# A chunk's results as running totals: 38 additions for 34, six PSUM copies for eight

## The chip, the cores and the metric

The kernel runs on one core of a Trainium2 chip. The metric is the device time of one execution in microseconds. The kernel before takes 1823.01 us, the median of three runs (1822.85 to 1823.12). Five engines of the core work side by side: TensorE (PE) multiplies matrices, VectorE (DVE) and ScalarE (ACT) work element by element and can read PSUM, GpSimd (POOL) works element by element in SBUF, and SyncE (SP) issues the DMAs.

## The reference, cut to what matters

```python
X = np.fft.fft(x, axis=1)          # x: 8 x 3008 x 256, float32
X = np.fft.fft(X, axis=2)
x = X.real.astype(np.float32).reshape(24064, 256)
h = x @ w_in                       # 256 -> 2048
g = np.maximum(0.01 * h, h)
return (g @ w_out).astype(np.float32)   # 2048 -> 256
```

## The kernel before, in words

The transform along the sequence is written with cosine and sine tables and folded by its symmetries. Each of the 8 batches gives two units, one with the odd and one with the even frequencies. The transform along the 256 features is folded into `w_in` (tensor `wf`). A unit is cut into two chunks of 188 or 189 pairs of columns; the first unit has one chunk of 125 pairs and is preceded by some plain pieces. So there are 31 chunks.

**Up.** A chunk takes 16 up steps, one for each block of 128 of the 2048 hidden features (`Chunk.up`, L1111). In a step TensorE makes a cosine product and a sine product (L1114) into the PSUM banks `cos_ps` and `sin_ps`, of which there are two each. ScalarE copies the cosine product (L1120) and writes the next start value into the bank (L1109). VectorE makes the sum and the difference of the two (L1127, two operations a step), which are the hidden values of both columns of a pair, and ScalarE applies the leaky ReLU (L1386).

**Down.** The product with `w_out` is not made block by block. Sums of hidden values (`SUMS`, L1144, on GpSimd or VectorE) are multiplied by sums of weights (`wt`, made once), as in fast matrix multiplication. A chunk has 26 products of four matmuls each (`PRODUCTS`, L1165); they accumulate to 24 values, numbered 0 to 23. Value a lies in half a % 2 of a PSUM bank, and a chunk fills 12 banks in order, in a ring of three (`sum_psa`, `sum_psb`, `sum_psc`). The products of a chunk run among the up steps of the next one.

**Results.** Eight results of 128 x 188 are signed sums of the 24 values. The table `COMBINED` lists additions `(x, y, sign)`. Entry i makes value 24 + i from two earlier ones; `RESULTS` names the eight that are stored. Values in `COPIED` are first copied from PSUM to SBUF by ScalarE (`combine`, L1181). All others are read by VectorE straight out of PSUM until their last use, and only then the bank is free. Every addition runs on VectorE (`make`, L1210) and writes to one of 24 slots of `part`. It has either two SBUF operands or one in PSUM.

**The order of the work.** It is fixed when the program is built. `rest` (L1298) sorts events by due time: up steps, sums and products. At each event `some` (L1331) hands out VectorE time from a budget in microseconds, first to the additions that are ready (`make_some`, L1223), and then to the folds of the next units' input and transform, which stand in one queue (`folds`, `Later.emit`, L983). The folds' operations have the lines L958, L960 and L978. An addition costs n / 960 + 0.07 of the budget. If products need a bank that still holds unread values, `leave` (L1194) emits the missing additions at once. A chunk's transform must be complete before its unit's first up step: `mixc` and `mixs` are the moving operands of L1114.

An addition from SBUF alone is also noted in `gate`. GpSimd's next sum is made to wait for the latest one noted (`wait_for_gate`, L1009).

The last chunk has its own tables, since none follows it.

Of the kernel before, what the change touches and what calls it, by code (L numbers as in the profile page):

```python
# [80 lines left out]
    (24, 7, 16), (25, 6, 17), (8, 39, 18), (13, 40, 19), (2, 8, 20), (1, 41, 21), (12, 42, 22), (5, 43, 23),  # L81
]
COMBINED = [
    (0, 12, -1), (20, 22, -1), (1, 10, 1), (6, 9, 1), (14, 19, -1), (11, 26, -1), (15, 27, 1), (3, 7, 1), (18, 24, 1),
    (12, 29, 1), (8, 31, 1), (25, 32, 1), (28, 34, 1), (2, 7, 1), (36, 20, 1), (38, 21, 1), (6, 4, -1), (40, 33, -1),
    (30, 3, -1), (42, 17, -1), (43, 25, -1), (13, 33, -1), (45, 36, -1), (14, 23, 1), (47, 35, 1), (1, 5, 1), (49, 37, 1),
    (50, 27, 1), (37, 30, 1), (52, 35, -1), (26, 0, -1), (54, 13, 1), (55, 16, -1), (56, 28, -1),
]
RESULTS = [39, 41, 44, 46, 48, 51, 53, 57]
COPIED = [0, 1, 2, 3, 4, 6, 14, 20]  # L90

LAST_COMBINED = [
    (0, 12, -1), (1, 10, 1), (6, 9, 1), (14, 19, -1), (11, 25, -1), (15, 26, 1), (3, 7, 1), (18, 24, 1), (12, 28, 1),
# [2 lines left out]
    (50, 27, -1), (14, 31, 1), (47, 31, -1), (41, 20, -1), (52, 20, 1), (53, 20, -1), (55, 22, -1), (54, 22, 1), (56, 22, 1),  # L96
    (57, 23, 1),
]
LAST_RESULTS = [37, 39, 58, 43, 60, 46, 59, 51]
NA = 24  # L100

# [193 lines left out]
def tile_fnet_leaky_relu(  # L295
# [792 lines left out]
    class Chunk:  # L1088
# [3 lines left out]
        def __init__(self, t):  # L1092
# [3 lines left out]
            self.last = t == len(chunk) - 1  # L1096
            self.combined, self.results = (LAST_COMBINED, LAST_RESULTS) if self.last else (COMBINED, RESULTS)
            self.sum_left = [0] * (NA + len(self.combined))
# [75 lines left out]
        def combine(self, bank):  # L1174

            n, here = self.n, [a for a in range(NA) if self.place(a)[0] == bank]
            for a in here:
                self.ready.add(a)
                if a in COPIED and not (self.last and a == 20):
                    self.copy[a] = part_of.take()  # L1180
                    nc.scalar.copy(part_of[self.copy[a]][:, 0:n], self.in_bank(a))  # L1181
                else:
                    self.held.add(a)
            for i, (x, y, _) in enumerate(self.combined):
                v = NA + i
                if v not in self.ready and x in self.ready and y in self.ready:
                    self.ready.add(v)
                    self.open.append(v)
# [446 lines left out]
```

## Time and profile before

| what | value |
|---|---|
| median of three runs | 1823.01 us |
| the profiled execution | 1822.73 us |
| its span, first to last instruction | 1820.9 us |
| TensorE busy | 1814.2 us |
| VectorE busy | 1550.7 us |
| ScalarE busy | 1124.1 us |
| GpSimd busy | 1081.9 us |
| additions, L1210 | 1057 on VectorE |
| copies, L1181 | 247 on ScalarE |

In the views of the profile, a row of a group gives line, engine, operation, what is written and read, shapes and count, then busy time, mean duration in ns, and the engine's idle time just before. A row of the timeline begins with start and duration in us, and ends with the count of merged instructions and, in brackets, an idle time and what ended it. In the waits, the numbers are the total in us, how often, and the longest. Each float32 matmul shows as two rows, since it is made in two passes, so 4712 matmuls give 9424 rows.

### The profile page before, as it was taken

To read this page: it belongs to the slowest core of one execution; us is meant where nothing else is said; L and a number is where in the kernel's file an instruction comes from. 1 tells how busy PE (TensorE), PEld (TensorE's weight loads), DVE (VectorE), ACT (ScalarE), POOL (GpSimd) and SP (SyncE) were. 2 spreads that over 40 slices of the span, in tenths; PEclk is the share of its full clock that TensorE was granted. 3 is DMA by queue.
4 is the path that set the end of the run, shared out by engine and by line. 5 is a ranking of instruction groups with operands and counts; after the bars stand their busy time and mean duration, and the time that the engine had idled before them with its cause. 6 is when DMAs were issued, how large, how long until landed. Compare 5 with 4: busy or idle time off the path is not lost.

```text
span 1820.9 us, 27090 instructions
## 1 busy us (share of the span) xinstructions
PE 1814.2 (100%) x9424; PEld 1543.4 (85%) x9424; DVE 1550.7 (85%) x3223; ACT 1124.1 (62%) x2297; POOL 1081.9 (59%) x587
## 2 busy tenths in 40 slices
PE   9999999999999999999999999999999999999999
PEld 7888888888888888888888888888888888888888
DVE  8979998897888978899787988879888798887678
ACT  4558666675666756566565666657666576565551
POOL 0246666565666665666665666656666666666660
PEclk9999999999999999999999999999999999999999
DMA  6312121202012011121101112010121110010000
GB/s 237 119 48 90 30 69 34 73 14 72 30 28 73 20 66 31 29 70 35 58 25 31 68 35 73 18 68 24 33 72 35 52 30 28 25 35 13 10 18 31
DMA packets 65897, 88.61 MB, mean 49 GB/s; under 512 B 10064, under 2 KB 53456, under 8 KB 65760
## 3 DMA queue, kind: packets, MB, share of 16 engines
q1 hardware_dynamic: 65616, 86.88, 14.5%
q8 instruction: 74, 1.21, 0.3%
q14 instruction: 63, 0.52, 0.1%
q10 hardware_dynamic: 144, 0.00, 0.0%
HBM read 62.12 MB, written 24.72 MB: 48 GB/s over the span
## 4 chain that ended last, share of the span: by engine, by line
PE 96%; DVE 2%; issue 0%; POOL 0%; DMA 0%; ACT 0%; DVEq 0%; POOLq 0%
PE sum_psc L1165 21%; PE sum_psa L1165 17%; PE sum_psb L1165 17%; PE cos_psa L1114 9%; PE sin_psa L1114 9%; PE sin_psb L1114 8%; PE cos_psb L1114 8%; PE dft_ps L713 3%; PE sum_psa L939 1%; PE sum_psb L939 1%; PE dft_ps L939 1%; PE sum_psc L939 1%; DVE block L1144 1%; PE sin_psb L901 0%; PE cos_psb L901 0%
## 5 line engine op out<-in xcount | busy, mean ns | idle before, releaser
L1144 POOL TENSOR_TENSOR block<-block 128x752 f32<-128x752 f32 (+2 forms) x540 | 1045.8, 1949 | 608.5 <-DVE xt L960 175.6
L1386 ACT ACTIVATE block<-block 128x376 f32<-128x376 f32 (+5 forms) x718 | 426.5, 623 | 3.9 <-DVE block L1127 3.2
L1144 DVE TENSOR_TENSOR block<-block 128x752 f32<-128x752 f32 (+2 forms) x328 | 417.4, 1276 | 0.2
L1127 DVE TENSOR_TENSOR block<-cos,sin_psa 128x376 f32<-128x376 f32 (+2 forms) x510 | 250.5, 531 | 141.6 <-PE sin_psa L1114 136.6
L1165 PEld LDWEIGHTS sum_psc<-block,wt 128*128 128x128 f32 x1736 | 289.3, 189 | 45.8 <-issue 0.5
L1165 PE MATMUL sum_psc<-block,wt 128*128 128x188 f32 (+2 forms) x1736 | 327.3, 321 | 0.4 <-DVE part L1210 0.4
L1127 DVE TENSOR_TENSOR block<-cos,sin_psb 128x376 f32<-128x376 f32 (+2 forms) x482 | 239.9, 538 | 101.1 <-PE sin_psb L1114 99.8
L1165 PE MATMUL sum_psa<-block,wt 128*128 128x188 f32 (+2 forms) x1736 | 312.1, 321 | 0.0
L1165 PEld LDWEIGHTS sum_psa<-block,wt 128*128 128x128 f32 x1736 | 283.4, 189 | 22.8
L1120 ACT COPY cos<-cos_psa 128x376 f32<-128x376 f32 (+2 forms) x255 | 119.0, 467 | 250.0 <-PE cos_psa L1114 247.2
L1120 ACT COPY cos<-cos_psb 128x376 f32<-128x376 f32 (+2 forms) x241 | 113.6, 471 | 210.8 <-PE cos_psb L1114 210.7
L1114 PE MATMUL cos_psa<-mixc,wf 128*128 128x376 f32 (+2 forms) x510 | 199.8, 473 | 0.5 <-ACT cos_psa L1109 0.5
L1114 PE MATMUL sin_psa<-mixs,wf 128*128 128x376 f32 (+2 forms) x510 | 199.7, 473 | 0.0
L1114 PE MATMUL sin_psb<-mixs,wf 128*128 128x376 f32 (+2 forms) x482 | 191.5, 479 | 0.0
L1114 PE MATMUL cos_psb<-mixc,wf 128*128 128x376 f32 (+2 forms) x482 | 191.4, 478 | 0.0
L1210 DVE TENSOR_TENSOR part<-part 128x188 f32<-128x188 f32 (+2 forms) x462 | 187.5, 442 | 1.8
L1165 PE MATMUL sum_psb<-block,wo 128*128 128x188 f32 (+2 forms) x992 | 188.0, 321 | 0.0
L1165 PEld LDWEIGHTS sum_psb<-block,wo 128*128 128x128 f32 x992 | 165.2, 189 | 22.8
L1165 PEld LDWEIGHTS sum_psb<-block,wt 128*128 128x128 f32 x992 | 163.5, 189 | 22.8
L1165 PE MATMUL sum_psb<-block,wt 128*128 128x188 f32 (+2 forms) x992 | 176.9, 321 | 0.0
L1109 ACT ACTIVATE cos_psa<-nb,wn 128x376 f32<-128x376 f32 (+2 forms) x255 | 146.0, 572 | 8.2
L1114 PEld LDWEIGHTS sin_psa<-mixs,wf 128*128 128x128 f32 x510 | 96.5, 189 | 61.8 <-DVE block L1127 0.4
(213 smaller groups left out, 1953.6 us busy)
## 6 DMA issues: line engine op xcount, KB each, us to landing
xt<-in_x_dram SPq DMA_DIRECT2D x28, 1024.0 KB, 5.3
out_dram<-part SPq DMA_DIRECT2D x176, 94.0 KB, 1.7
out_dram<-part SPq DMA_DIRECT2D x64, 94.5 KB, 1.7
tabe<-in_seq_tab_dram SPq DMA_DIRECT2D x29, 190.0 KB, 2.6
nb<-nyq_dram SPq DMA_DIRECT2D x23, 188.0 KB, 3.8
block<-in_w_in_dram SPq DMA_DIRECT2D x8, 512.0 KB, 5.4
block<-in_w_out_dram SPq DMA_DIRECT2D x8, 512.0 KB, 4.6
xt<-in_first_x_dram SPq DMA_DIRECT2D x4, 768.0 KB, 7.9
```

Source lines behind the costliest of these rows:

```text
L713: nc.tensor.matmul(o, lhsT=still, rhs=moving, start=(i == 0), stop=(i == 3), skip_group_check=True)
L939: nc.tensor.matmul(sums[j][d][:, r * n : (r + 1) * n], lhsT=wo[:, fs[h] // 4, fs[h] % 4, d], rhs=a[r][h], start=(f == 0 and r == 0 and h = ...
L1109: nc.scalar.activation(cos_ps[self.half(f)][:, 0 : self.w], columns_of(nb_sb, self.u, self.j, self.w), ACT.Copy, scale=wn[:, f : f + 1])
L1114: nc.tensor.matmul(bank[:, 0 : self.w], lhsT=wf[:, i, f * P : (f + 1) * P], rhs=columns_of(mix_sb[i], self.u, self.j, self.w), start=(i == ...
L1120: nc.scalar.copy(copy, cos[:, 0 : self.w])
L1127: nc.vector.tensor_tensor(block.row(to, g, self.n), x, y, op=op)
L1144: ins = (engine or nc.gpsimd).tensor_tensor(self.value(16 + i), xa, ya, op=ALU.add if sign > 0 else ALU.subtract)
L1165: nc.tensor.matmul(to, lhsT=weight(w)[:, g], rhs=self.value(v)[:, g], start=(first and at == 0), stop=(last and g == 3), skip_group_check= ...
L1210: ins = nc.vector.tensor_tensor(part_of[self.copy[v]][:, 0:n], xa, ya, op=ALU.add if sign > 0 else ALU.subtract)
L1386: nc.scalar.activation(to, to, ACT.Lrelu)
```

## The change

The tables for all chunks but the last are replaced. Before, partial sums are made first and combined late, 15 of the 34 additions from SBUF alone. After, a partial total runs along the banks and takes up each value as it comes: 38 additions, of which 8 are from SBUF alone. Values 6 and 20 are no longer copied. The last chunk keeps its additions and its copies, which now have a list of their own.

```diff
 COMBINED = [
-    (0, 12, -1), (20, 22, -1), (1, 10, 1), (6, 9, 1), (14, 19, -1), (11, 26, -1), (15, 27, 1), (3, 7, 1), (18, 24, 1),
-    (12, 29, 1), (8, 31, 1), (25, 32, 1), (28, 34, 1), (2, 7, 1), (36, 20, 1), (38, 21, 1), (6, 4, -1), (40, 33, -1),
-    (30, 3, -1), (42, 17, -1), (43, 25, -1), (13, 33, -1), (45, 36, -1), (14, 23, 1), (47, 35, 1), (1, 5, 1), (49, 37, 1),
-    (50, 27, 1), (37, 30, 1), (52, 35, -1), (26, 0, -1), (54, 13, 1), (55, 16, -1), (56, 28, -1),
+    (1, 5, 1), (4, 6, -1), (3, 6, -1), (2, 6, 1), (3, 7, 1), (27, 7, 1), (28, 8, 1), (26, 9, -1), (29, 9, 1),
+    (24, 32, 1), (1, 10, 1), (34, 11, -1), (30, 11, 1), (12, 0, -1), (35, 12, -1), (36, 12, 1), (38, 25, -1), (34, 13, 1),
+    (30, 14, 1), (41, 14, -1), (15, 31, -1), (32, 15, 1), (0, 16, 1), (17, 44, -1), (37, 18, -1), (42, 19, -1), (43, 19, 1),
+    (50, 39, -1), (50, 46, -1), (20, 48, -1), (49, 20, 1), (47, 20, 1), (54, 21, 1), (22, 53, -1), (22, 55, -1), (45, 57, 1),
+    (14, 23, 1), (60, 57, -1),
 ]
-RESULTS = [39, 41, 44, 46, 48, 51, 53, 57]
-COPIED = [0, 1, 2, 3, 4, 6, 14, 20]
+RESULTS = [56, 40, 58, 51, 61, 33, 59, 52]
+COPIED = [0, 1, 2, 3, 4, 14]
...
+LAST_COPIED = [0, 1, 2, 3, 4, 6, 14]
...
-                if a in COPIED and not (self.last and a == 20):
+                if a in (LAST_COPIED if self.last else COPIED):
```

From the two inserted lines on, line numbers of the changed kernel are larger by two (L1127 becomes L1129, L1210 becomes L1212).

## The prediction, made before the result was known

> **What bounds the kernel now.** I read the page's shares and chain first, then the busy time by stages, TensorE's waits, the VectorE groups, and the timeline around each of those waits.
>
> ```profile
> PE 1814.2 (100%) x9424; PEld 1543.4 (85%) x9424; DVE 1550.7 (85%) x3223; ACT 1124.1 (62%) x2297; POOL 1081.9 (59%) x587
> PE 96%; DVE 2%; issue 0%; POOL 0%; DMA 0%; ACT 0%; DVEq 0%; POOLq 0%
> ```
>
> TensorE carries 96% of the chain; VectorE is full to 85% and carries 2%. Busy time by stages:
>
> ```profile
> 178.00:188.00 10.00, 9.14 (x54) 7.27 (x54) 9.88 (x22) 8.42 (x21) 7.48 (x5) 1.00 0.00 0
> 188.00:1786.00 1598.00, 1598.00 (x8337) 1363.73 (x8336) 1357.41 (x2826) 1008.00 (x2082) 1015.97 (x519) 1.00 0.13 41
> 1786.00:1796.00 10.00, 9.51 (x59) 8.93 (x58) 10.00 (x17) 1.39 (x5) 0.00 (x0) 1.00 0.11 33
> ```
>
> First column TensorE, third VectorE. Between 188 and 1786 us no time is missing. In the trace's rows the starts agree: 128x188 passes follow each other every 0.16 us (two passes a product), 128x376 passes every 0.315 us, and no start in this stretch is over 0.06 us late. TensorE's own waits, whole run:
>
> ```profile
> PE sum_psa L1165 <- DVE part L1210: 0.5, 1, 0.5
> PE sum_psc L1165 <- DVE block L1144: 0.4, 1, 0.4
> PE sum_psc L1165 <- DVE part L1210: 0.4, 1, 0.4
> ```
>
> (Three more, 2.1 us, lie before the first chunk's additions.) By start to start, the stalls that these additions can reach are: 181 us, 0.52+0.07 (restart); 185 us, 0.67+0.10; 1788.9 us, 0.37; 1793 us, 0.65. Sum 2.4 us. This is all that a better order of the additions could win.
>
> [...]
>
> ```profile
> L1210 DVE TENSOR_TENSOR part<-part 128x188 f32<-128x188 f32 (+2 forms) x462 | 187.5, 442 | 1.8
> L1210 DVE TENSOR_TENSOR part<-part,sum_psc 128x188 f32<-128x188 f32 (+2 forms) x187 | 58.3, 339 | 0.0
> ```
>
> 442 ns with both inputs in SBUF, 339 with one in PSUM. [...]
>
> **The change, part by part.** Steady state first; I counted operations from the two tables.
>
> Additions: before, 19 with a PSUM operand and 15 from SBUF alone; after, 30 and 8. By the rows, 19x0.339+15x0.442 = 13.1 us a chunk; 30x0.339+8x0.442 = 13.7 us: +0.6 us. Durations overlap, so by start to start: four more at 0.26 (two in line take 0.60, one 0.34) is +1.05 us, less contention and less dependence (an addition right behind the one it needs starts 0.38 after it, and the changed order has 77 such pairs in the run for 118). I take +0.3 us a chunk, bounds -0.5 and +1.1. VectorE has (1598-1357)/29 = 8.3 us free a chunk, so nothing of this reaches the end by its sum. Only a bank freed too late can.
>
> Banks: by the starts and ends in the trace, from 204 us to the tail almost all reopened sum banks have at least 2.4 us between the last VectorE reader's end and the first product; the closest has 1.4. I went through the changed program's instruction order and added up VectorE work against TensorE time from each pair of L1127 (the two operations that tie VectorE to the up step). The lag moves by some tenths. The closest place in the steady part is a product that needs a VectorE sum (L1144), once per two units: 2.8 us before, 1.2 us after. Above nothing, so 0 us; if uncovered it would cost its shortfall, six times. Nothing is forced: no addition is emitted only because a bank is reopened.
>
> Copies: two fewer on ScalarE (L1181), 0.31 us each, 0.6 us a chunk. ScalarE waits 458 us on the cos products, which hides it: 0 us. GpSimd keeps its order; its sums wait less for SBUF additions (89.5 us now), and TensorE never waits for them: 0 us. SP issues the same eight stores a chunk, some a step earlier or later: 0 us. The last chunk keeps its tables.
>
> What is left is three single places. The additions also share a time budget with the transform's folds, so a different count moves these folds between steps.
>
> Head. Before:
>
> ```profile
> 180.88 0.47 DVE L1210 TENSOR_TENSOR part<-part,sum_psc 128x125 f32<-128x125 f32 x2
> 181.27 0.59 DVE L978 SCALAR_TENSOR_TENSOR xt<-xt,angle,dft_ps 95x128 f32<-95x128 f32 x2
> 181.95 1.98 DVE L1144 TENSOR_TENSOR block<-block 128x756 f32<-128x756 f32 x1
> 183.85 0.99 DVE L1127 TENSOR_TENSOR block<-cos,sin_psb 128x378 f32<-128x378 f32 x2
> 184.76 0.27 DVE L1210 TENSOR_TENSOR part<-part,sum_psa 128x125 f32<-128x125 f32 x1
> 184.96 0.27 DVE L1210 TENSOR_TENSOR part<-sum_psa,part 128x125 f32<-128x125 f32 x1
> ```
>
> Chunk 1's first products wait for the last of these (185.29). In the changed order the step that begins at 179.96 has one PSUM fold of 512 and one SBUF fold of 512 (0.60 each) where the two L978 (0.26 each) stood: +0.68. A third reader of bank a is added: +0.20. VectorE arrives about 0.08 earlier. So that wait ends 0.8 us later: +0.8 us. Up to 198 us the lag is 1.3 to 2.2 us over before's, and the spans there (0.33 us at 189.85, 0.37 at 191.76, 1.1 at 199) fall short by at most 0.3 us; the 0.8 already lost covers that.
>
> Third unit's first sine product. Before:
>
> ```profile
> 237.41 1.00 DVE L960 TENSOR_TENSOR mixs<-ev,od 128x376 f32<-128x376 f32 x2
> 238.34 1.00 DVE L1127 TENSOR_TENSOR block<-cos,sin_psb 128x376 f32<-128x376 f32 x2
> 240.27 0.79 PE L1114 MATMUL sin_psa<-mixs,wf 128*128 128x376 f32 x2
> ```
>
> mixs is ready at 237.96 (first half), 2.3 us early. In the changed order the four operations that make it come one up step later, behind L1127 x2 (0.92), three PSUM additions (0.79), two L958 (0.53) and two SBUF additions (0.53); its first half takes 0.55. Sum 3.3, from 0.27 after the previous sine product's last pass gave way: 3.6 us, against 3.50-0.63 = 2.87 us to the next sine product. Wait 0.7, with the semaphore 0.06: +0.8 us. Between 0 (if VectorE came a step earlier by more than I count) and +2.4 (if each SBUF operation meets a GpSimd one, as the 1.98 us row shows).
>
> Tail. Before:
>
> ```profile
> 1788.20 0.60 DVE L1210 TENSOR_TENSOR part<-part,sum_psc 128x189 f32<-128x189 f32 x2
> 1788.72 1.15 DVE L1210 TENSOR_TENSOR part<-part 128x189 f32<-128x189 f32 x4
> 1788.86 1.54 PE L1165 MATMUL sum_psc<-block,wo 128*128 128x188 f32 x8
> ```
>
> VectorE works without a break from 1776.73. Up to these two readers the changed order has two more additions (+0.52), up to the L1144 that ends the 1793 us stall one more (+0.26). The stalls, 0.37 and 0.65 now, become 0.89 and 0.39: +0.3 us. After that the chain is TensorE alone, then the same last addition and store.
>
> Sum: 0+0.8+0.8+0.3 = +1.9 us. The profiled execution took 1822.73 (span 1820.9 and 1.8 around it), so 1824.6; the median of the runs is 0.28 higher, so 1824.9.
>
> **Rivals.** (1) *Faster*: the different additions end the head and tail waits. At most 2.4 us, 1820.6; the saved contention speaks for it, the longer rows in front of both waits against. Even whole it is under 0.2% (3.6 us, about what a measurement of this kernel can tell from no change). (2) *Slower, by a bank wait in every chunk*: five PSUM readers stand in a row where four stood, and a bank is reopened before the last is done. It decides where VectorE is more than 2.4 us later than now; each 0.2 us over costs 0.2x29 = 5.8 us, 1830.7. For it: VectorE at 85%, and single rows of 2.65 us under GpSimd. Against it: the 8.3 us free a chunk, and that PSUM readers avoid those rows. (3) *Only the middle place is sized wrong*: with contention at 2.4, the sum is +3.5, 1826.5; with two contended rows in the head as well, 1827.5. (4) *Nothing moves*: the folds shift without meeting a wait, 1823.0.
>
> **How the numbers follow.** Forecast (+1 to +3 us) 0.6; (4) and smaller 0.17; (1) 0.05; (3) 0.1, half of it over 3.6 us; (2) 0.08. Faster by over 0.2% can't come from 2.4 us of stalls: 0.01. Slower: 0.08+0.05, 0.13. Same: 0.86. The range of 8 in 10 leaves out (1)'s and (2)'s ends: 1822.4 to 1827.6.
>
> **What would show it.** In the changed profile: TensorE still without a gap between 242 and 1786 us; a wait of TensorE on the L962 mixs (L960 before) near 241 us of some 0.5 to 0.8 us; the wait on part near 185 us longer by 0.8; the 1788.9 us wait longer and the 1793 us one shorter; ScalarE's L1183 copies 187 for 247; 442 ns of SBUF additions less. I am wrong if TensorE waits for L1212 repeatedly in the steady part, or if the head's stalls shrink.

## The result and the profile after

| | before | after |
|---|---|---|
| median, 22 runs each | 1823.01 us (1822.70 to 1823.60) | 1826.26 us (1824.92 to 1827.06) |
| ratio after / before | | 1.0017, 95% interval 1.0011 to 1.0023 |
| profiled execution, span | 1822.73, 1820.9 us | 1825.13, 1823.3 us |
| additions on VectorE, copies on ScalarE | 1057, 247 | 1177, 187 |

The changed kernel is 0.17% slower. The executions lie at two heights: eleven of the 22 took 1824.92 to 1825.75 us at a mean granted TensorE clock of 1.000 (the share of full clock that the profile records), eleven took 1826.76 to 1827.06 us at 0.999, and the median is the middle of the gap between them. The kernel before has no such gap. The profiled execution belongs to the lower eleven, so its trace explains 2.4 us of the 3.25; the other part had to be looked for by experiment.

First the page of the changed kernel: the engines' busy times, and the shares of the chain of work that ended last.

```profile
PE 1814.2 (100%) x9424; PEld 1544.0 (85%) x9424; DVE 1590.0 (87%) x3343; ACT 1105.8 (61%) x2237; POOL 1089.4 (60%) x587
PE 96%; DVE 3%; issue 0%; DMA 0%; POOL 0%; ACT 0%; DVEq 0%; POOLq 0%
```

VectorE has 39.3 us more to do (1550.7 before) and ScalarE 18.3 us less, yet TensorE's busy time is the same 1814.2 us. So the 2.4 us are idle time of TensorE. Where it lies is read from the busy time by stages of the changed kernel (start and end in us, length, then TensorE, weight loads, VectorE, ScalarE, GpSimd, the granted clock, DMA share and GB/s):

```profile
180.00:190.00 10.00, 8.73 (x52) 7.28 (x51) 10.00 (x24) 7.14 (x18) 8.26 (x5) 1.00 0.07 19
238.00:248.00 10.00, 8.04 (x42) 6.68 (x42) 9.36 (x20) 4.86 (x10) 7.25 (x4) 1.00 0.11 32
248.00:1786.00 1538.00, 1538.00 (x8016) 1311.86 (x8015) 1341.47 (x2821) 955.00 (x1951) 984.08 (x499) 1.00 0.13 41
1786.00:1797.00 11.00, 10.44 (x65) 10.01 (x64) 11.00 (x21) 1.07 (x4) 0.00 (x0) 1.00 0.17 54
```

From 248 to 1786 us TensorE is again without a gap: twenty-seven chunks run on the new tables and cost nothing. The stretch from 238 to 248, where the kernel before had 10.00 us of TensorE, has 8.04. TensorE's own waits on these places, in the changed kernel:

```profile
PE sin_psa L1116 <- DVE mixs L962: 2.0, 1, 2.0
PE sum_psa L1167 <- DVE part L1212: 1.3, 1, 1.3
PE sum_psc L1167 <- DVE part L1212: 0.6, 1, 0.6
```

One wait is new, on `mixs`. By start to start of TensorE's rows, which counts the restart after a wait too, the stalls are:

| place | before | after | difference | forecast |
|---|---|---|---|---|
| head, 181 and 185 us | 0.59 + 0.77 | 0 + 1.53 | +0.17 | +0.8 |
| third unit's first sine product, 240 us | 0 | 2.22 | +2.22 | +0.8 |
| 248 to 1786 us | 0 | 0 | 0 | 0 |
| tail, 1789 and 1793 us | 0.37 + 0.65 | 0.83 + 0.10 | -0.09 | +0.3 |
| sum | 2.4 | 4.7 | +2.3 | +1.9 |

The sum agrees with the spans, 1823.3 less 1820.9.

**The middle place.** VectorE's and TensorE's timeline of the changed kernel, and GpSimd's sums beside it:

```profile
233.94 7.73 POOL L1146 TENSOR_TENSOR block<-block 128x752 f32<-128x752 f32 x4 [0.95 <-DVE block L1146]
...
235.77 2.51 DVE L1146 TENSOR_TENSOR block<-block 128x752 f32<-128x752 f32 x1 [0.38 <-POOL block L1146]
238.20 0.99 DVE L1129 TENSOR_TENSOR block<-cos,sin_psb 128x376 f32<-128x376 f32 x2
239.11 0.86 DVE L1212 TENSOR_TENSOR part<-part,sum_psa 128x189 f32<-128x189 f32 x3
239.90 0.72 DVE L960 TENSOR_TENSOR od<-e,dft_ps 128x188 f32<-128x188 f32 x2
240.53 1.61 DVE L1212 TENSOR_TENSOR part<-part 128x189 f32<-128x189 f32 x2
242.06 0.99 DVE L962 TENSOR_TENSOR mixs<-ev,od 128x376 f32<-128x376 f32 x2
...
242.66 0.90 PE L1116 MATMUL sin_psa<-mixs,wf 128*128 128x376 f32 x2 [1.96 <-DVE mixs L962]
```

The four operations that make `mixs` stand one up step later, behind L1129, three PSUM additions and two SBUF additions, as the forecast listed them. What it had wrong is durations. GpSimd works on four sums in a row, 233.94 to 241.67, in this place (the kernel before has two, with a break of 2.15 us between 236.41 and 238.56). Beside them the VectorE sum L1146 takes 2.51 us (0.94 in the kernel before at 236.56), so that L1129 starts 0.26 us later than the product it needs would allow; and the two SBUF additions take 1.61 us instead of the some 0.6 of a free pair (0.62 for two at 1785.88 in the changed kernel's own tail, where GpSimd is idle). The two L960 take 0.63 to the next start, where 0.53 was counted. The forecast's 0.8 plus 0.26, 1.0 and 0.1 is 2.2, the stall by starts in the table; the view, which leaves out the restart, shows 2.0. All three PSUM additions beside the same GpSimd work took 0.86, their normal time (0.87 for three at 1786.67, where GpSimd is idle). In the whole kernel before, no addition with a PSUM operand took more than 357 ns, and one from SBUF alone took up to 1830. That SBUF additions are contended at this time stood already in the kernel before's timeline, where four of them took 3.19 us beside GpSimd's sums of 238.56 to 242.22 (four take 1.15 at 1788.72, where GpSimd is idle):

```profile
239.77 3.19 DVE L1210 TENSOR_TENSOR part<-part 128x189 f32<-128x189 f32 x4
```

**The head.** The changed kernel's timeline:

```profile
181.42 1.98 DVE L1146 TENSOR_TENSOR block<-block 128x756 f32<-128x756 f32 x1
183.32 0.68 DVE L962 TENSOR_TENSOR xt<-xt 128x512 f32<-128x512 f32 x1
183.92 0.99 DVE L1129 TENSOR_TENSOR block<-cos,sin_psb 128x378 f32<-128x378 f32 x2
184.84 0.66 DVE L1212 TENSOR_TENSOR part<-part,sum_psa 128x125 f32<-128x125 f32 x3
...
185.55 0.59 PE L1167 MATMUL sum_psa<-block,wo 128*128 128x189 f32 x2 [1.27 <-DVE part L1212]
```

The fold of 512 (0.60 to the next start) and the third reader (0.20) are there, as forecast. But L1146 starts at 181.42, where it started at 181.95: VectorE came 0.53 us earlier, not 0.08 (it is as far ahead already at 176.46, for 176.99). The last reader ends at 185.50 for 185.23. TensorE, whose wait at 181 us is gone, came to the bank earlier and waits there longer, and what it gained at the first wait it gives back at the second.

**The tail.** In the changed kernel's timeline TensorE waits once and not twice:

```profile
1791.79 1.54 PE L1167 MATMUL sum_psc<-block,wo 128*128 128x188 f32 x8 [0.56 <-DVE part L1212]
...
1795.73 1.54 PE L1167 MATMUL sum_psc<-block,wo 128*128 128x188 f32 x8
```

**The steady part.** VectorE's groups of the changed kernel, SBUF additions first:

```profile
L1212 DVE TENSOR_TENSOR part<-part 128x188 f32<-128x188 f32 (+2 forms) x252 | 123.1, 519 | 1.5
L1212 DVE TENSOR_TENSOR part<-part,sum_psa 128x188 f32<-128x188 f32 (+2 forms) x336 | 94.6, 341 | 0.9 <-PE sum_psa L1167 0.9
```

There are 252 SBUF additions for 462, but one takes 519 ns on average for 442; additions from PSUM stay near 340. VectorE has 1.3 us more a chunk (39.3 over 30 chunks), still far inside its 8.3 us free. Only 0.8 of this is the additions (L1212 is busy for 387.5 us, L1210 was for 363.8). The folds of the transform with both inputs in SBUF grew by 28.8 us (L962 177.1, L960 before 148.4), with the same operations; one group of them took 348 ns a row before:

```profile
L962 DVE TENSOR_TENSOR ev<-ab 128x188 f32<-128x188 f32 x28 | 21.2, 798 | 0.2
```

VectorE's own sums, L1146, took 12.4 us less (405.0 for 417.4). So, to judge by the durations, the contention did not go with the SBUF additions; part of it moved to the folds.

### The profile page after: what moved, and what is told of

Same layout as the page of the kernel before. It is cut to its first block, busy times and chain, and to the rows that moved or that the text cites. A ratio compares the mean times of both kernels' runs of the same rounds, so it can differ in the third digit from the quotient of the medians.

```text
span 1823.3 us, 27127 instructions
## 1 busy us (share of the span) xinstructions
PE 1814.2 (100%) x9424; PEld 1544.0 (85%) x9424; DVE 1590.0 (87%) x3343; ACT 1105.8 (61%) x2237; POOL 1089.4 (60%) x587
## 4 chain that ended last, share of the span: by engine, by line
PE 96%; DVE 3%; issue 0%; DMA 0%; POOL 0%; ACT 0%; DVEq 0%; POOLq 0%
PE sum_psc L1167 21%; PE sum_psa L1167 17%; PE sum_psb L1167 17%; PE sin_psa L1116 9%; PE cos_psa L1116 9%; PE sin_psb L1116 8%; PE cos_psb L1116 8%; PE dft_ps L715 3%; PE sum_psa L941 1%; PE sum_psb L941 1%; PE dft_ps L941 1%; PE sum_psc L941 1%; DVE block L1146 1%; DVE part L1212 1%; DVE block L1129 1%; PE cos_psb L903 0%
## 5 line engine op out<-in xcount | busy, mean ns | idle before, releaser
L1146 POOL TENSOR_TENSOR block<-block 128x752 f32<-128x752 f32 (+2 forms) x540 | 1054.2, 1966 | 602.9 <-DVE xt L962 173.6
L1146 DVE TENSOR_TENSOR block<-block 128x752 f32<-128x752 f32 (+2 forms) x328 | 405.0, 1238 | 3.7 <-POOL block L1146 3.6
L1129 DVE TENSOR_TENSOR block<-cos,sin_psa 128x376 f32<-128x376 f32 (+2 forms) x510 | 250.9, 533 | 121.6 <-PE sin_psa L1116 116.9
L1129 DVE TENSOR_TENSOR block<-cos,sin_psb 128x376 f32<-128x376 f32 (+2 forms) x482 | 240.0, 538 | 82.7 <-PE sin_psb L1116 82.1
L1111 ACT ACTIVATE cos_psb<-nb,wn 128x376 f32<-128x376 f32 (+2 forms) x241 | 139.3, 578 | 7.9
```

The lines of the kernel that those rows point to most:

```text
L1111: nc.scalar.activation(cos_ps[self.half(f)][:, 0 : self.w], columns_of(nb_sb, self.u, self.j, self.w), ACT.Copy, scale=wn[:, f : f + 1])
L1129: nc.vector.tensor_tensor(block.row(to, g, self.n), x, y, op=op)
L1146: ins = (engine or nc.gpsimd).tensor_tensor(self.value(16 + i), xa, ya, op=ALU.add if sign > 0 else ALU.subtract)
```

## The experiments

Theory A: the loss is the one late `mixs`, which the time budget's order puts a step later in the third chunk; half of the executions lose a further 1.6 us as a consequence of that wait of TensorE. Rival: the tables cost time in every chunk (the 39 us of VectorE), or the extra 1.6 us belong to the changed order elsewhere. Runs of the kernel before beside the first four runs have a median of 1822.90 us, and beside the later ones 1822.90 and 1822.92.

**One number of the budget.** `SHARES` scales the VectorE time that `some` hands out; its first number holds up to step 33, in the first three chunks.

```diff
-SHARES = (0.9, 1.2)
+SHARES = (0.95, 1.2)
```

> The changed kernel with one constant changed: the budget per step before step 34 is 0.95 instead of 0.9. In the instruction order this brings the third unit's mixs one up step earlier and changes no table. Theory A (the cost is the one wait for mixs near 240 us, and the second level at 1827 comes from this wait too): no wait on mixs, one level only, 1823.2 (1822.8 to 1823.8), from a head that is some 0.3 us slower than before's and a tail 0.1 faster. Rival B (the changed order of the additions costs in the steady part, or makes the second level): the two levels near 1825.3 and 1826.9 stay, less at most the mixs wait.

Measured: 1823.29 us (1823.00 to 1823.65), ratio 1.0002 (0.9993 to 1.0010), and no execution apart from the others. TensorE has 10.00 us in 238 to 248; the wait on `mixs` is gone. VectorE's timeline of this kernel:

```profile
234.24 1.00 DVE L962 TENSOR_TENSOR mixs<-ev,od 128x376 f32<-128x376 f32 x2
...
237.21 2.52 DVE L1146 TENSOR_TENSOR block<-block 128x752 f32<-128x752 f32 x1 [0.35 <-POOL block L1146]
...
241.46 1.88 DVE L1212 TENSOR_TENSOR part<-part 128x189 f32<-128x189 f32 x1
```

`mixs` is made 6 us before it is needed. The contended rows are still there, 2.52 and 1.88 us, and cost nothing where they stand: contention sets how large the wait is, the order sets whether there is one. With all tables changed the time is, within the interval, that of the kernel before (0.4 us above it by the medians), so the tables as such cost nothing that these runs can tell.

**The new tables in the first three chunks alone, and everywhere else alone.**

```diff
-            self.combined, self.results = (LAST_COMBINED, LAST_RESULTS) if self.last else (COMBINED, RESULTS)
+            old = t >= 3      # the other kernel: t < 3
+            self.combined, self.results, self.copied = (
+                (LAST_COMBINED, LAST_RESULTS, LAST_COPIED) if self.last else
+                (OLD_COMBINED, OLD_RESULTS, OLD_COPIED) if old else (COMBINED, RESULTS, COPIED))
```

> The kernel before, with the new tables for the first three chunks alone. Theory A: the same as the changed kernel, 1825.0 to 1827.2 in two levels 1.6 apart, with a wait of 1.5 to 2.5 us on mixs near 240 us, though 28 of 31 chunks are the old ones. Rival B: 1823.0 to 1823.6, one level.

> The changed kernel with the old tables for the first three chunks alone. Theory A: 1822.9 (1822.6 to 1823.2), one level, waits at 181 and 185 us as before, none near 240 us, the tail 0.1 faster. Rival B: 1825 to 1827 in two levels, since 27 chunks have the new tables.

Measured: with the new tables in chunks 0 to 2 alone, 1825.77 us, ratio 1.0017 (1.0010 to 1.0023), again at two heights (thirteen from 1825.13 to 1825.90, eight from 1826.69 to 1827.16), with the same wait of 2.0 us on `mixs`. With them in all other chunks but the last, 1822.82 us, ratio 1.0000 (0.9991 to 1.0008), no wait on `mixs`, no second height. Three chunks carry the whole loss, the second height included; twenty-seven carry none. The gain of the second kernel in the tail (0.93 us of stalls for 1.02) is too small to see, and no version tried beats the kernel before.

**A late `mixs` in the kernel before.** After up step 47, VectorE makes one of the two `od` additions again several times and then the first half of `mixs` once, writing the same values. All else is the kernel before.

```diff
+                again[:] = [
+                    lambda: nc.vector.tensor_tensor(four(od)[:, 0::3], two(o0, 1, n, n), two(po, q + 1, n, n), op=ALU.add),
+                    lambda: nc.vector.tensor_tensor(lo_to[0:m, 0:kw], ev[0:m, 0:kw], od[0:m, 0:kw], op=ALU.add)]
...
+                if 16 * t + i == 47:
+                    for _ in range(10):     # 4, 7, 13, 18 in the others
+                        again[0]()
+                    again[1]()
```

> The kernel before, where after up step 47 VectorE repeats ten times an addition that makes od (0.26 each, same values), and then the first half of mixs, so that the third unit's first sine product comes about 2.2 us late. No table is changed. Theory A, second half (a single wait of TensorE of about 2 us costs itself, and in about half of the executions 1.6 us more through the granted clock): 1825.2 and 1826.8, two levels. Rival C (the second level has another source in the changed order): 1825.2, one level.

> The kernel before, with the work ahead of the third unit's first sine product lengthened by 4 repeated VectorE operations (the same values written again) instead of 10. By the row of the ten-fold run (3.4 us of wait, 0.2 us for a repeat) the wait on mixs should be 1.9 to 2.2 us, as long as the changed kernel's 2.1. Theory A (a wait of TensorE of this length is followed in part of the executions by a stretch at a lower granted clock, whatever made the wait): two levels as in the changed kernel, about 1825.0 and about 1826.6 us, the upper with a mean clock of 0.999. Rival B (only the wait counts; the second level belongs to the changed order): one level, 1824.8 to 1825.3 us.

> The same with 18 repeats: a wait of about 5.2 us. Theory A with a share that grows with the wait: a lower level near 1828.8 us and more than half of the executions above it, by 1.6 us or more, at a clock of 0.999 or less. Rival B: one level, 1828.4 to 1829.2 us, clock 1.000. Rival C (the level is a matter of the execution, not of the wait's length): half of the executions 1.6 us above the other half.

> 13 repeats, for a profile between the 10-fold one (wait 3.3 us, no half-clock stretch) and the 18-fold one (6.3 us, a half-clock stretch of 6.8 us). Wait 4.2 to 4.8 us. Theory A [...]: a stretch of 3.4 us at half clock, or 6.8, with products at 0.31 us for 0.16 after the wait, 1.5 to 2.4 us in sum, time 1828.0 + 1.6 or so = 1829.5 us. Rival (half clock only for a wait of more than 5 us): clock 1.00 throughout, 1828.0 us.

> 7 repeats: wait about 2.7 us. Theory A: 1825.7 to 1826.0 us without, 1827.3 to 1827.6 us with a half-clock stretch of 3.4 us; with one, its products show the 1.6 us. Rival: no such stretch, 1825.8 us.

| repeats | wait on `mixs`, profiled | half clock after it, profiled | time, us |
|---|---|---|---|
| 4 | 2.1 us | none | 1825.48, ratio 1.0016 (1.0010 to 1.0023); 13 runs from 1825.04 to 1825.85, 8 from 1826.78 to 1827.21 |
| 7 | 2.1 us | 3.41 us | 1826.96, one run |
| 10 | 3.3 us | none | 1827.06, ratio 1.0025 (1.0015 to 1.0036); 5 runs from 1826.88 to 1827.11, and 1828.08, 1828.49, 1829.26 |
| 13 | 4.4 us | 3.41 us | 1829.74, one run |
| 18 | 6.3 us | 6.83 us | 1831.47, ratio 1.0047 (1.0034 to 1.0059); 5 runs from 1831.23 to 1831.99 |

The half clock is read from the trace's record of the granted clock. The tenfold kernel was meant to wait 2.2 us and waited 3.3; the fourfold one has the changed kernel's wait. The wait with seven repeats was expected at 2.7 us. It came out as 2.1, as with four: there the repeated half of `mixs` met a GpSimd sum and took 1.71 us, here it began as that sum was ending (242.07, the sum's row ends at 242.24) and took 0.57. So these two kernels have the same wait, and one profile with a half-clock stretch and one without. The same two stretches of time in the four-fold kernel:

```profile
240.00:242.60 2.60, 0.53 (x2) 0.00 (x0) 2.50 (x5) 1.90 (x4) 2.17 (x2) 1.00 0.00 0
242.60:247.40 4.80, 4.76 (x24) 4.00 (x25) 4.77 (x11) 1.24 (x3) 2.86 (x2) 1.00 0.19 61
```

and in the seven-fold one:

```profile
240.00:242.60 2.60, 0.57 (x2) 0.00 (x0) 2.39 (x8) 1.90 (x4) 2.23 (x2) 1.00 0.00 0
242.60:247.40 4.80, 4.71 (x16) 4.33 (x17) 4.47 (x11) 0.00 (x0) 2.80 (x2) 0.64 0.19 61
```

TensorE seems busy in both, 4.76 and 4.71 us, but with 24 rows in the one and 16 in the other, at a granted clock of 1.00 and 0.64. The seven-fold kernel's timeline shows the pace:

```profile
242.69 0.90 PE L1119 MATMUL sin_psa<-mixs,wf 128*128 128x376 f32 x2 [2.12 <-DVE mixs L801]
243.43 0.78 PE L1170 MATMUL sum_psc<-block,wt 128*128 128x189 f32 x2
244.00 2.73 PE L1170 MATMUL sum_psc<-block,wo 128*128 128x189 f32 x8
```

The fourfold kernel's has for the same eight passes:

```profile
243.69 1.44 PE L1170 MATMUL sum_psc<-block,wo 128*128 128x189 f32 x8
```

Eight passes take 2.73 us for 1.44. Start to start they follow each other 0.31 us apart instead of 0.16, ten times, and two more are late in part: 1.7 us, half of the 3.41. The two heights lie 1.6 us apart in the changed kernel and 1.7 in the fourfold one, by their medians. The seven-fold execution took 1826.96 us, among the upper eleven of the changed kernel. So the kernel with the old tables and a wait of the same length has the two heights too, and theory A holds. The rival that half clock needs a wait of over 5 us falls with the seven- and thirteen-fold kernels; with 18 repeats, where an equal share at both heights was one of the rivals, all five runs have a clock of 0.998. The expected lower height of 1828.8 us was missed: the wait was 6.3 and not 5.2, and none stayed without half clock.

**Profiles of further executions of the changed kernel**, which could have lain among the upper ones.

> The changed kernel once more, for a profile of an execution of the upper level. If this execution lies there (about 1826.9 us), theory A expects TensorE's products just after the wait at 242 us to follow each other at half pace for some us, 1.6 us in sum, and no other new wait; the rival expects the 1.6 us in another place, a wait that the lower level's profile does not have. If it lies on the lower level (about 1825.2 us), it repeats the known profile.

> As the look before: the changed kernel once more, for a profile of the upper level; half pace after the wait at 242 us by theory A, another wait by the rival.

> The changed kernel once more, for a profile of the upper level: with a chance of one in two a half-clock stretch of 3.4 us just after 242 us and 1826.9 us; else 1825.2 us and clock 1.00.

Measured: 1825.05, 1825.87 and 1825.60 us, all three with the known 2.0 us wait, and no half clock after it (a mean clock of 1.000 in each). So the stretch was not seen in a trace of the changed kernel itself. For it, that the upper eleven are due to such a stretch rests on their mean clock of 0.999, on the distance of 1.6 us, and on the seven-fold kernel.

**What decides it in one execution.** The length of the wait alone does not: with 3.3 us of wait, the tenfold kernel has a mean clock under 1.000 in 3 of 8 runs, with 2.1 us the fourfold kernel in 8 of 21, and of the two profiled waits of 2.1 us one was followed by half clock and one was not. The seven-fold kernel has, 0.8 us after its wait,

```profile
243.48:246.89 3.41, 3.41 (x13) 3.41 (x12) 3.41 (x7) 0.00 (x0) 2.29 (x2) 0.50 0.27 85
```

and the tenfold one, whose longer wait ends at 244.52,

```profile
244.00:246.00 2.00, 1.48 (x7) 1.23 (x8) 1.97 (x7) 0.00 (x0) 0.00 (x0) 1.00 0.00 0
246.00:248.00 2.00, 2.00 (x12) 1.74 (x11) 2.00 (x5) 0.00 (x0) 1.66 (x1) 1.00 0.31 97
248.00:250.00 2.00, 2.00 (x12) 1.75 (x11) 2.00 (x4) 1.80 (x3) 1.92 (x2) 1.00 0.15 48
```

The granted clock is 0.50 in the one and 1.00 in the other. What decides it was not shown, and why the tenfold kernel has a clock under 1.000 in only 3 of 8 runs stays open.

## Why the prediction was right, and which of its terms were not

**The result as a whole.** The forecast was 1824.9 us, no measurable change, for the likeliest case; the median is 1826.26, inside the range, and the sum of +1.9 us stands against +2.3 in the profile. The total agrees better than its terms do: the head was taken 0.6 too high, the tail 0.4 too high and the middle 1.4 too low, and the half clock, which no term had, moves the median by another 0.9 or so. That so much cancels is luck. The forecast also took changes below 3.6 us as too small to tell from none; over 22 runs each, 3.25 us is told clearly (interval 1.0011 to 1.0023).

**Steady state at 0: right.** No wait on an addition between 248 and 1786 us, and the kernel with the new tables in those chunks alone measured 1.0000. The cost hidden there was undersized, 0.8 us a chunk for the additions where 0.3 was taken, and 1.3 in all. The term that failed is "less contention": fewer SBUF additions were taken to mean less contention at 442 ns each, but those that are left took 519 ns on average, and the folds beside them grew by 28.8 us, for which there was no term. The cover of 8.3 us made it harmless.

**Head, +0.8: its mechanism seen, its sum wrong.** The folds cost 0.60 (0.68 forecast) and the third reader 0.20, and the wait at 185 us grew by 0.76. That this is near the forecast's 0.8 is chance: 0.27 of it is VectorE ending later, the rest TensorE arriving 0.5 earlier. The step that failed is that VectorE "arrives about 0.08 earlier": it came 0.53 earlier, which ended the wait at 181 us. TensorE then comes to the second wait earlier by as much. The forecast treated 0.52 + 0.07 as staying and added the 0.8 to it; two waits in a row on the same late engine must be added up by when VectorE ends, which was 0.27 later (185.50 for 185.23). Of this 0.10 was there already: in this profile TensorE's rows at 180 us lie 0.10 later than before (180.19 for 180.09). That leaves the 0.17 of the table.

**Middle place, +0.8: place and mechanism right, size wrong by 1.4.** The wait is on the operand that was named, in the step that was named. Its upper bound of 2.4, put down to meeting GpSimd, was nearly reached, and with the wait gone, in the share-of-budget experiment, 0.4 us of slowdown are left, which is within the interval. The term at fault is "two SBUF additions (0.53)", with VectorE on time at L1127. They took 1.61, behind an L1146 of 2.51 us. GpSimd's timing was taken from the kernel before, with its break; in the changed one the sums closed up, and L1146 fell among them. The two additions would have met GpSimd with the break too: the four at 239.77 in the kernel before did. "Two L958 (0.53)" is a smaller slip, 0.64 to the next start in the kernel before. Rival (3), contended at 2.4 us, is what the trace shows in this place; that the median is also near its 1826.5 is chance, since the half clock is no part of it.

**Tail, +0.3: wrong by 0.4.** The first wait grew as said (0.37 to 0.83, forecast 0.89), but the second ended (0.10 of restart, forecast 0.39). The term that failed is "one more (+0.26)" up to the sum that ends it. From the L1127 at 1776.73 (L1129 at 1779.20 after) to the start of VectorE's last run of sums (1789.78, after 1792.17) it took 13.05 us before and 12.97 after, although there are 16 additions for 15. Before, four SBUF additions in a row from 1783.15 took 1.37 us to the next start, 0.33 more than four at 0.26.

**Copies, SP, GpSimd at 0: right in effect.** 60 copies fewer are 18.3 us less of ScalarE, and no wait moved with them. Rivals (1) and (2) did not happen: the head's and tail's waits sum to what they were, within 0.1 us (two of the four ended, and the other two grew), and no bank is late in the steady part.

**What no term had:** the 1.6 us more of eleven of the 22 executions, at a mean clock of 0.999, put down above to half clock after the wait. It makes up the rest of the 3.25 us, since the median lies in the gap between the heights. The forecast priced a wait at its own length.

## What to carry to other kernels

Where a kernel's order comes from a time budget, a change that costs nothing in the steady part can still push one operand a step too late in a single place; look for such places by name in the built order, and price them with whatever GpSimd is doing beside them (here 1.61 us for two SBUF additions, 0.62 where it is idle), not with the mean row. A nudge of the budget (0.9 to 0.95 here) took back all but 0.4 us of the loss, so try it before rejecting the change. And do not price a wait of TensorE at its length alone: with the one of 2.0 us here, eleven of 22 executions took 1.6 us more than the others, at a mean granted clock of 0.999 for 1.000.

## What the runs showed of the hardware that was not expected

A single wait of TensorE of 2.1 us, in a stream otherwise without a gap from 188 to 1786 us, was followed by 3.41 us at a granted clock of 0.50 in the seven-fold kernel's profile, and by none in the four-fold one's. 8 of 21 executions of the latter lie 1.7 us above its others, and eleven of 22 of the changed kernel 1.6 us, all at a mean clock of 0.999 for 1.000. After 4.4 us of wait there was one stretch of 3.41 us, after 6.3 us one of 6.83, part of which fell into the wait, and after 3.3 us none in the profiled execution. What makes the difference these runs do not show.
